# A planner's slots, stores and clock in a fused attention and feed-forward kernel

## The chip, the cores and the metric

The kernel runs on one core of a Trainium2 chip. The metric is the device time of one execution in microseconds (us). The engines are TensorE (PE, matrix products, with PEld for its weight loads), VectorE (DVE), ScalarE (ACT), GpSimd (POOL, which has next to nothing to do here) and SyncE (SP), which issues the DMA transfers; SPq in the profile is SP's queue.

## The reference

```python
S = 448; D = 64                            # 8 batches, 12 heads
scores = q @ k.T / sqrt(D) - log(S)
attn = (1 / (1 + exp(-scores))) @ v        # a sigmoid, no row sum
x = attn, heads side by side               # 3584 tokens x 768
h = max(x @ w_in, 0)                       # w_in: 768 x 2048
g = s * h * h + b                          # s, b: one number each
out = g @ w_out                            # w_out: 2048 x 768
```

Everything is fp32.

## The kernel before, in words

Each fp32 factor of a product is split into a high part and a rest (the low part), both in TensorE's rounded format fp32r, and a product takes three matmuls: high x high, high x low, low x high. The high part is a copy that rounds (ACT, line 1340 for g, 547 for a weight block); the low part is a subtraction from the unrounded value (DVE, through the helper at line 421; 418 is the helper for additions).

The program has three stages in time.

1. Attention, 0 to about 250 us. While it runs, weights are loaded and converted to fp32 blocks (wf), sums over weight blocks are made, and some of them are rounded into tiles t_l_f_g (group g of the row sums of weight block f in layer l) and stored to HBM (wd, line 563 for a base block, 1401 for row sums).
2. The plain block, about 250 to 385 us: the first 512 tokens in the plain form. There are 16 blocks f of 128 hidden channels, taken in the order 0, 8, 1, 9, ... 7, 15. The first layer of a block (ph, line 818, function ffn1, 18 matmuls) and the second layer (po, line 1271, function ffn2, 18 matmuls) alternate on TensorE, each booked with HALF = 4.09 us. Between the two stands the activation: ACT makes r from ph (three passes) and rounds it to g, DVE makes g's low part. Beside this work, the rounded blocks w_l_f (layer l, block f) and the row sums t_0_f_g are made by ACT and DVE and stored by SP, since the third stage reads them back.
3. The fast block, about 385 to 1022 us: the other 6 x 512 tokens, in two groups of three, by a bilinear scheme that needs fewer products and more sums. A unit is 12 matmuls with one set of weights (wu), loaded from wd in HBM (line 918); a_n_mk are tokens, loaded from xd (line 575). Its products (b, lines 1009 and 1018) take operands o_, split into o_..h and o_..l; wr are weight rows that are read back, summed and stored again.

The order of the instructions in the plain block is not written out by hand. A Planner (lines 250 to 325) holds operations, each with an engine, an expected time, the operations it comes after, a number of slots that it needs, and a `late` time. `lag` is how long after its own time an operation counts as done; for a store that is the expected time until it has landed. `deadlines` pulls each `late` forward from its successors. `run` then simulates the engines' clocks: at each step the engine with the earliest possible start takes, of the operations that can start within 0.25 us of one another, the one with the smallest `late`. The result is a fixed order per engine. The chip keeps to it, and waits by semaphores where the real times differ. The planner's clock counts from the start of the plain block: `plan1.clock.update(...)` says when each engine comes free then.

Tiles of first-layer blocks and row sums come from a heap of slots, cx (8 slots "c" and 5 slots "t"). A slot is freed in the plan with a time (`cx.free(tile, at + ...)`), and the next tile takes the slot that stands first in the list. On the chip the first write to a new tile waits until the last reader of the old tile is done, stores among the readers. Second-layer blocks come instead from a ring p2 of three tiles: block i takes the place of block i-3. The plan makes its rounding (ACT) come after the ffn2 of block i-3, and says nothing of that block's store.

`keep` issues the store of a base block. A first-layer tile has two uses (`uses`): its product and its store. Its slot is freed by whichever comes last. `left` (line 1441) does what attention left over on DVE: the low parts of three tiles t_1_1_4, t_1_1_5 and t_1_1_6 (row sums of a second-layer block), and their stores.

At the end of the plain block (the seam) the pools of stages 1 and 2 are closed, and 32 slots of equal size open over the same memory for the fast block. `old` lists the regions of the closed pools with the count at which each was last freed; `h2` orders the 32 new slots by the largest count of the regions below them, so that the first tiles of the fast block go to places that have long been free. In `old` the regions are, in order: 8 slots "c", 4 half-size tiles, 2 small tiles, the 3 tiles of the ring p2, 3 of g, and the 5 slots "t".

Of the kernel before, what the change touches and what calls it, by code (L numbers as in the profile page):

```python
# [36 lines left out]
TB = 512  # L37
# [9 lines left out]
AHEAD_1, AHEAD_R = 16.0, 40.0  # L47
# [281 lines left out]
def sigmoid_attention_relu2_ffn(  # L329
# [17 lines left out]
    KW = DM // 3  # L347
# [10 lines left out]
    def pool(stack, name, bufs, side=None, space=None):  # L358
        kw = dict(side=side) if side else {}
        if space is not None:  # L360
            kw["space"] = space
        return stack.enter_context(
            tc.tile_pool(name=name, bufs=bufs, reuse_waits="tile", **kw)
        )
# [28 lines left out]
    cx = Slots(pool(first, "cx", 1), 8, "c")  # L393
# [3 lines left out]
    early = ExitStack()  # L397
# [16 lines left out]
    def f32(ap):  # L414
        return ap.bitcast(F32)
# [45 lines left out]
    def block(l, f, n):  # L461

        if l == 0:
            return wf[0][f + int(n[1]) * NQ4][:, int(n[0])]
        return wf[1][f + int(n[0]) * NQ4][:, int(n[1])]
# [75 lines left out]
    def base_hi(l, f):  # L541
        shape = [P, 3, 2, KW]
        if l:
            t = p2.tile(shape, F32R, tag="w", name=f"w_{l}_{f}")
        else:
            t = cx.tile(shape, F32R, name=f"w_{l}_{f}")
        nc.scalar.copy(t[:, :, 0], wf[l][f])
        return t

    def base_lo(l, f, t):  # L550
        sub(t[:, :, 1], wf[l][f], f32(t[:, :, 0]))

    def base_rows(l, f):
        part = f // NQ4
        names = [f"{part}{k}" if l else f"{k}{part}" for k in range(3)]
        return [x for x in names if x in ROWS[l]], [k for k in range(3) if names[k] in ROWS[l]]

    def base_store(l, f, t):
        names, thirds = base_rows(l, f)
        f %= NQ4  # L560
        step = thirds[-1] - thirds[0] if len(thirds) == 2 else 1
        row, n = ROWS[l].index(names[0]), len(thirds)
        nc.sync.dma_start(
            wd[l][f // 2][:, row : row + n, f % 2],
            f32(t[:, thirds[0] : thirds[-1] + 1 : step]).rearrange("p k h c -> p k (h c)"),
        )
        kept.update((l, x, f) for x in names)
# [14 lines left out]
    at = ExitStack()  # L582
# [207 lines left out]
    pieces, late = iter(pieces[:-LATE]), pieces[-LATE:]  # L790
# [123 lines left out]
    def fetch():  # L914
        n, l, row, p = stream[len(fetched)]
        assert {(l, row, 2 * p), (l, row, 2 * p + 1)} <= kept, (l, row, p)
        t = roll.tile([P, 2, 2, KW], F32R, tag="wu", name=f"wu_{len(fetched)}")
        nc.sync.dma_start(f32(t).rearrange("p j h c -> p j (h c)"), wd[l][p][:, ROWS[l].index(row)])
        fetched.append(t)
# [332 lines left out]
    for a, *_ in PRODUCTS_1:  # L1252
        seen = [a]
        while seen:
            x = seen.pop(0)
            d = {s_[0]: (s_[1], s_[3]) for s_ in SUMS_1}.get(x)
# [21 lines left out]
    plan1 = Planner(cx)  # L1278
    HALF = 4.09
    w_t, w_lo, g_t, acts, ffns, ph_t = {}, {}, {}, {}, {}, {0: ph0}  # L1280
    row_op, readers, nearly = {}, [], []

    def due(i, l):
        return max(0.0, min(2 * i - 1 + 3 * l, 2 * NF - 1) * HALF)

    def weights(l, i):
        f = order[i]
        uses = [2 - l]

        def drop(at):  # L1290
            uses[0] -= 1
            if not uses[0]:
                cx.free(w_t[l, i], at)

        def run_hi(at):
            w_t[l, i] = base_hi(l, f)

        def keep(at):
            base_store(l, f, w_t[l, i])
            if not l:  # L1300
                drop(at + 5.0)

        h = plan1.op("ACT", 0.76, [ffns.get((1, i - 3))] if l else [], run_hi, 1 - l, early=AHEAD_1)
        d = plan1.op("DVE", 0.89, [h], lambda at: base_lo(l, f, w_t[l, i]))
        k = plan1.op("SP", 0.64 * len(base_rows(l, f)[0]), [d], keep, lag=4.0, late=due(i, l) + 10.0)
        for r in base_rows(l, f)[0]:
            row_op[l, r, f % NQ4] = k
        if f % NP < NP - 1:
            readers.extend((h, d))
        w_lo[l, i] = d, drop  # L1310
# [56 lines left out]
    def weight_sums(f):  # L1367
        tiles = {}

        def new_tile(g):  # L1370
            tiles[g] = cx.tile([P, 3, 2, KW], F32R, name=f"t_0_{f}_{g}")
            return tiles[g]

        jobs = row_sums(0, f, 3, new_tile, lambda x: (lambda: block(0, f, x)), lambda *a: None)
        a, b = ROWS_DUE[f]
        names = [SUM_ROWS[0][k : k + 3] for k in range(0, len(SUM_ROWS[0]), 3)]
        chain = [conv.get(f + NP - NQ4), conv.get(f + NF - NQ4)]
        total = sum(j[1] for j in jobs)
        fresh, his, spent = [], {}, 0.0
        for kind, time, g, fn in jobs:  # L1380
            spent += time
            if kind == "new":
                fresh.append(fn)
            elif kind == "hi":
                his[g] = plan1.op("ACT", 0.04 + 0.24 * len(names[g]), chain, lambda at, fn=fn: fn())
            elif kind == "sum":
                def run(at, fn=fn, first=tuple(fresh)):
                    for x in first:
                        x()
                    fn()  # L1390

                o = plan1.op("DVE", 0.36, chain, run, len(fresh), early=AHEAD_R)
                if f < NQ4 - 1:
                    readers.append(o)
                fresh, chain = [], [o]
            else:
                o = plan1.op("DVE", time, [his[g]] + chain, lambda at, fn=fn: fn())

                def keep(at, g=g):
                    row = ROWS[0].index(names[g][0])  # L1400
                    nc.sync.dma_start(
                        wd[0][f // 2][:, row : row + len(names[g]), f % 2],
                        f32(tiles[g][:, : len(names[g])]).rearrange("p k h c -> p k (h c)"),
                    )
                    cx.free(tiles[g], at + 6.0)
                    kept.update((0, r, f) for r in names[g])

                k = plan1.op("SP", 0.64 * len(names[g]), [o], keep, lag=4.0, late=a + (b - a) * spent / total)
                for r in names[g]:
                    row_op[0, r, f] = k  # L1410
# [3 lines left out]
    for i in range(NF):  # L1414
        weights(1, i)
        if i:
            weights(0, i)
            first_ffn(i)
        activation(i)
        if i:  # L1420
            second_ffn(i - 1)
# [13 lines left out]
    x = None  # L1435
    for k in range(AHEAD):
        _, l, row, p = stream[k]
        after = [o, x] + [row_op.get((l, row, f)) for f in (2 * p, 2 * p + 1)]
        x = plan1.op("SP", 1.28, after, lambda at: fetch(), late=OPEN_DUE + 6.0 + 2.8 * k)
# [5 lines left out]
        stores.clear()  # L1445

    if (NL, "DVE") in plan:
        plan1.op("DVE", 2.4, [], left, late=12.0)
    plan1.full = False
    plan1.clock.update(PE=0.0, DVE=1.0, ACT=-1.0, SP=1.0)  # L1450
    plan1.deadlines()
    plan1.run()
    assert not plan
# [9 lines left out]
    blk.close()  # L1463
    first.close()
    old, at = [], 0
    for tags, size in (("c", 8), 6 * KW), ((None, 4), 3 * KW), ((None, 2), TB), ((None, 3), 6 * KW), ((None, 3), 2 * TB), (("t", 5), 6 * KW):
        for i in range(tags[1]):
            old.append((at, at + size, cx.used[f"{tags[0]}{i}" + "_0" * (tags[0] == "t")] if tags[0] else 0))
            at += size
    size = 2 * TB  # L1470
    h2 = sorted(range(32), key=lambda i: max([u for a, b, u in old if a < (i + 1) * size and b > i * size] or [0]))
# [50 lines left out]
```

## Time and profile before

| | us |
|---|---|
| median of three runs | 1025.07 (1024.07 to 1028.45) |
| the profiled execution | 1024.43 |
| its span | 1022.6 |
| PE busy | 1013.6 (99%) |
| DVE busy | 882.1 (86%) |
| ACT busy | 717.4 (70%) |
| HBM traffic | 272 GB/s over the span |

Busy times are sums over instructions of one engine; the rest of the span is idle time of that engine. In rows of instructions, the first two numbers are start and length in us, then come the engine, the line, the operation, output<-inputs, the shape, and in brackets the idle time just before and what ended it. "DMA wd<-w" as a releaser means that a store of a w tile landed. Rows of a DMA give the time of issue and the time to the landing.

### The profile page before, as it was taken

What the parts mean: (1) busy time and instruction counts of PE and PEld (TensorE: products, weight loads), DVE (VectorE), ACT (ScalarE), POOL (GpSimd) and SP (SyncE); (2) the same over time, 40 slices, a digit from 0 to 9 for tenths busy, and PEclk for the clock granted to TensorE, in tenths of its full rate; (3) what the DMA queues carried; (4) which work ended last, traced back from release to release, by engine and by line L of the source; (5) the groups of instructions that cost most, each with busy time, mean ns of one, the idle gap of its engine ahead of it and who ended that gap; (6) DMA issues with size and microseconds to landing.
All of it is one profiled execution on the core that took longest, in us unless ns stands there. A gap on an engine that the chain in (4) does not pass through costs nothing.

```text
span 1022.6 us, 13811 instructions
## 1 busy us (share of the span) xinstructions
PE 1013.6 (99%) x5194; PEld 761.8 (74%) x5194; DVE 882.1 (86%) x989; ACT 717.4 (70%) x772; POOL 0.2 (0%) x4
## 2 busy tenths in 40 slices
PE   9999999999999999999999999999999999999998
PEld 4545454555788878887887888888888887888887
DVE  5899999998999938989979999899767678999997
ACT  7889999999777747737898954424655889964421
POOL 0000000000000000000000000000000000000000
PEclk9999999999999999999999999999999999999999
DMA  8788999895997998998876666799776666666675
GB/s 338 265 307 300 334 336 391 307 377 222 385 408 308 354 403 303 380 330 275 266 237 186 189 200 189 224 354 326 222 210 194 195 190 189 199 188 199 209 226 186
DMA packets 101073, 278.77 MB, mean 273 GB/s; under 512 B 10000, under 2 KB 23184, under 8 KB 101008
## 3 DMA queue, kind: packets, MB, share of 16 engines
q1 hardware_dynamic: 100720, 277.45, 79.5%
q8 instruction: 41, 0.67, 0.3%
q10 hardware_dynamic: 288, 0.46, 0.1%
q14 instruction: 24, 0.20, 0.1%
HBM read 193.99 MB, written 83.89 MB: 272 GB/s over the span
## 4 chain that ended last, share of the span: by engine, by line
PE 90%; DVE 4%; DMA 3%; ACT 2%; issue 1%; SPq 1%; ACTq 0%; DVEq 0%
PE b L1018 31%; PE b L1009 27%; PE pav L692 10%; PE psc L658 8%; PE po L1271 5%; PE ph L818 4%; PE psc_l L679 2%; PE pav L701 2%; DVE t L421 1%; DVE r L418 1%; DMA wr<-wr 1%; DMA wd<-w 1%; DMA wd<-t 1%; ACT a L638 1%; DVE w L421 0%
## 5 line engine op out<-in xcount | busy, mean ns | idle before, releaser
L1009 PE MATMUL b<-o_0h,wu 128*128 128x512 f32 x928 | 286.5, 389 | 0.7 <-DVE r L421 0.7
L1009 PEld LDWEIGHTS b<-o_0h,wu 128*128 128x128 f32 x928 | 174.2, 188 | 37.9 <-DVE r L421 1.6
L1009 PE MATMUL b<-o_0l,wu 128*128 128x512 f32 x464 | 180.7, 389 | 1.6 <-DVE o_0l L421 1.6
L1018 PE MATMUL b<-o_0h,wu 128*128 128x512 f32 x464 | 152.4, 389 | 0.0
L1018 PE MATMUL b<-o_1h,wu 128*128 128x512 f32 x456 | 149.6, 389 | 0.0
L638 ACT ACTIVATE a<-psc,nls 128x896 f32<-128x896 f32 x144 | 132.7, 1010 | 12.8 <-PE psc L658 10.4
L692 PE MATMUL pav<-a,v 128*64 128x448 f32 x576 | 113.8, 543 | 0.0
L418 DVE TENSOR_TENSOR r<-r,b 128x1024 f32<-128x1024 f32 x74 | 89.4, 1217 | 27.5 <-PE b L1009 17.9
L421 DVE TENSOR_TENSOR r<-r,b 128x1024 f32<-128x1024 f32 x66 | 80.1, 1217 | 25.8 <-PE b L1009 17.0
L1009 PEld LDWEIGHTS b<-o_0l,wu 128*128 128x128 f32 x464 | 87.1, 188 | 19.9 <-DVE o_0l L421 2.0
L1018 PEld LDWEIGHTS b<-o_0h,wu 128*128 128x128 f32 x464 | 87.1, 188 | 18.3 <-ACT r L1064 0.3
L1018 PEld LDWEIGHTS b<-o_1h,wu 128*128 128x128 f32 x456 | 85.6, 188 | 17.9
L1018 PE MATMUL b<-o_0l,wu 128*128 128x512 f32 x232 | 90.3, 389 | 0.0
L1018 PE MATMUL b<-o_1l,wu 128*128 128x512 f32 x228 | 88.7, 389 | 0.0
L692 PEld LDWEIGHTS pav<-a,v 128*64 128x64 f32 x576 | 39.1, 137 | 63.9 <-issue 45.1
L959 ACT CAST o_0h<-r 128x1024 fp32r<-128x1024 f32 x26 | 27.1, 1052 | 67.9 <-DVE r L421 40.0
L1271 PE MATMUL po<-g,w 128*128 128x512 f32 x288 | 68.6, 390 | 2.5 <-ACT g L1340 1.6
L1064 ACT ACTIVATE r<-b 128x1024 f32<-128x1024 f32 x46 | 46.4, 1027 | 31.2 <-DVE r L418 13.8
L1271 PEld LDWEIGHTS po<-g,w 128*128 128x128 f32 x288 | 53.9, 188 | 14.8 <-ACT g L1340 2.0
L491 ACT CAST t<-t 128x768 fp32r<-128x768 f32 (+2 forms) x62 | 44.3, 732 | 29.0 <-DVE t L421 21.7
L818 PE MATMUL ph<-x0h,w 128*128 128x512 f32 x192 | 61.7, 390 | 0.0
L1138 ACT ACTIVATE r<-r,b_sb,s_sb 128x1024 f32<-128x1024 f32 x48 | 59.6, 1243 | 1.0
(115 smaller groups left out, 1693.2 us busy)
## 6 DMA issues: line engine op xcount, KB each, us to landing
wu<-wd SPq DMA_DIRECT2D x232, 512.0 KB, 4.2
wd<-t SPq DMA_DIRECT2D x36, 768.0 KB, 7.0
qk<-qk_t SPq DMA_DIRECT2D x23, 896.0 KB, 6.9
st<-w_out SPq DMA_DIRECT2D x16, 768.0 KB, 8.9
st<-w_in SPq DMA_DIRECT2D x16, 768.0 KB, 9.3
wd<-t SPq DMA_DIRECT2D x22, 512.0 KB, 5.1
v<-v_t SPq DMA_DIRECT2D x24, 448.0 KB, 5.3
xd<-xo SPq DMA_DIRECT2D x24, 448.0 KB, 3.8
```

Source lines behind the costliest of these rows:

```text
L418: nc.vector.tensor_tensor(o, x, y, op=ALU.add)
L421: nc.vector.tensor_tensor(o, x, y, op=ALU.subtract)
L491: nc.scalar.copy(ts[g][:, :n, 0], f32(ts[g][:, :n, 1]))
L638: nc.scalar.activation(a, psc[:, :, :S], AF.Sigmoid, bias=nls, scale=SCALE)
L658: nc.tensor.matmul(o[:, j, :S], two[wi][r, i, cols], two[xi][r, i, :S], start=m == 0, stop=m == 2,)
L692: nc.tensor.matmul(pav[r, i, :S], ld_[1][:, 3 * i + c, j, :], a[i, c][:, j, :], start=c == 0, stop=False,)
L818: nc.tensor.matmul(ph, w[:, k, wi, kc * P : (kc + 1) * P], x0[h][xi][:, cc, :], start=m == 0, stop=m == 3 * NCC - 1,)
L1009: nc.tensor.matmul(bk[:, j], wt[:, j, wi, c * P : (c + 1) * P], tiles[xi][:, c, :], start=first and m == 0, stop=m == 3 * KC - 1, skip_gro ...
L1018: nc.tensor.matmul(bk[:, e], wt[:, f, wi, e * P : (e + 1) * P], tiles[gi][:, f], start=first and f == 0 and m == 0, stop=p == np_ - 1 and ...
L1064: nc.scalar.activation(v.t, bank_t[b], AF.Copy, scale=-1.0)
L1138: nc.scalar.activation(v.t, v.t, AF.Identity, bias=b_sb, scale=s_sb)
L1271: nc.tensor.matmul(pos[e], w[:, k, wi, kc * P : (kc + 1) * P], g[:, gi, :], start=first and i == 0, stop=last and i == 2,)
```

## The change

It changes numbers and dependences of the plain block's planner, and the order in which the places at the seam are taken.

- `keep` of a base block: the store counts as landed 8 us after its issue, not 4. A first-layer tile whose last use is its store is booked as free 8 us after it, not 5. The `late` time of a second-layer store is the block's due time itself, not 10 us later.
- The rounding of second-layer block i comes also after the store of block i-3 (`stored_1`).
- Tiles of row sums are booked as free 8 us after their store, not 6.
- `left` has `late` 20 us, not 12.
- The planner's clock starts with DVE free at 2.8 us and ACT at 0.1, not 1.0 and -1.0.
- At the seam, the three regions of p2 count as freed last of all (tag -1).

```diff
@@ -1278,7 +1278,7 @@
     plan1 = Planner(cx)
     HALF = 4.09
     w_t, w_lo, g_t, acts, ffns, ph_t = {}, {}, {}, {}, {}, {0: ph0}
-    row_op, readers, nearly = {}, [], []
+    row_op, readers, stored_1 = {}, [], {}
 
     def due(i, l):
         return max(0.0, min(2 * i - 1 + 3 * l, 2 * NF - 1) * HALF)
@@ -1298,11 +1298,14 @@
         def keep(at):
             base_store(l, f, w_t[l, i])
             if not l:
-                drop(at + 5.0)
-
-        h = plan1.op("ACT", 0.76, [ffns.get((1, i - 3))] if l else [], run_hi, 1 - l, early=AHEAD_1)
+                drop(at + 8.0)
+
+        before = [ffns.get((1, i - 3)), stored_1.get(i - 3)] if l else []
+        h = plan1.op("ACT", 0.76, before, run_hi, 1 - l, early=AHEAD_1)
         d = plan1.op("DVE", 0.89, [h], lambda at: base_lo(l, f, w_t[l, i]))
-        k = plan1.op("SP", 0.64 * len(base_rows(l, f)[0]), [d], keep, lag=4.0, late=due(i, l) + 10.0)
+        k = plan1.op("SP", 0.64 * len(base_rows(l, f)[0]), [d], keep, lag=8.0, late=due(i, l) + 10.0 * (1 - l))
+        if l:
+            stored_1[i] = k
         for r in base_rows(l, f)[0]:
             row_op[l, r, f % NQ4] = k
         if f % NP < NP - 1:
@@ -1402,7 +1405,7 @@
                         wd[0][f // 2][:, row : row + len(names[g]), f % 2],
                         f32(tiles[g][:, : len(names[g])]).rearrange("p k h c -> p k (h c)"),
                     )
-                    cx.free(tiles[g], at + 6.0)
+                    cx.free(tiles[g], at + 8.0)
                     kept.update((0, r, f) for r in names[g])
 
                 k = plan1.op("SP", 0.64 * len(names[g]), [o], keep, lag=4.0, late=a + (b - a) * spent / total)
@@ -1445,9 +1448,9 @@
         stores.clear()
 
     if (NL, "DVE") in plan:
-        plan1.op("DVE", 2.4, [], left, late=12.0)
+        plan1.op("DVE", 2.4, [], left, late=20.0)
     plan1.full = False
-    plan1.clock.update(PE=0.0, DVE=1.0, ACT=-1.0, SP=1.0)
+    plan1.clock.update(PE=0.0, DVE=2.8, ACT=0.1, SP=1.0)
     plan1.deadlines()
     plan1.run()
     assert not plan
@@ -1463,9 +1466,11 @@
     blk.close()
     first.close()
     old, at = [], 0
-    for tags, size in (("c", 8), 6 * KW), ((None, 4), 3 * KW), ((None, 2), TB), ((None, 3), 6 * KW), ((None, 3), 2 * TB), (("t", 5), 6 * KW):
-        for i in range(tags[1]):
-            old.append((at, at + size, cx.used[f"{tags[0]}{i}" + "_0" * (tags[0] == "t")] if tags[0] else 0))
+    for tag, n, size in (("c", 8, 6 * KW), (0, 4, 3 * KW), (0, 2, TB), (-1, 3, 6 * KW), (0, 3, 2 * TB), ("t", 5, 6 * KW)):
+        for i in range(n):
+            names = (f"{tag}{i}", f"{tag}{i}_0")
+            used = cx.count + 1 if tag == -1 else sum(cx.used[x] for x in names)
+            old.append((at, at + size, used))
             at += size
     size = 2 * TB
     h2 = sorted(range(32), key=lambda i: max([u for a, b, u in old if a < (i + 1) * size and b > i * size] or [0]))
```

TensorE's order is the same in both kernels, and so is the number of instructions on every engine. The following rows are in each engine's order of issue (line, operation, output<-inputs, shape).

DVE at the start of the plain block, before. The wf tiles are unrounded weight blocks, w_0_1 is a rounded one, g_0 the activation of the first block.

```order
L421 TENSOR_TENSOR w_0_1_2736<-wf_0_1_102,w_0_1_2736 128x3x256
L421 TENSOR_TENSOR t_0_0_0_2746<-wf_0_4_114,wf_0_12_116 128x256
L421 TENSOR_TENSOR t_1_1_5_2579<-t_1_1_5_2579 128x3x256
L421 TENSOR_TENSOR t_1_1_4_2479<-t_1_1_4_2479 128x3x256
L421 TENSOR_TENSOR t_1_1_6_2583<-t_1_1_6_2583 128x256
L421 TENSOR_TENSOR t_0_0_0_2746<-wf_0_8_100,wf_0_12_116 128x256
L418 TENSOR_TENSOR t_0_0_0_2746<-t_0_0_0_2746 128x256
L421 TENSOR_TENSOR g_0_2774<-r_0_2775,g_0_2774 128x512
```

The same place, after:

```order
L421 TENSOR_TENSOR w_0_1_2736<-wf_0_1_102,w_0_1_2736 128x3x256
L421 TENSOR_TENSOR t_0_0_0_2771<-wf_0_4_114,wf_0_12_116 128x256
L421 TENSOR_TENSOR t_0_0_0_2771<-wf_0_8_100,wf_0_12_116 128x256
L418 TENSOR_TENSOR t_0_0_0_2771<-t_0_0_0_2771 128x256
L421 TENSOR_TENSOR t_0_0_0_2771<-wf_0_0_98,t_0_0_0_2771 128x256
L421 TENSOR_TENSOR t_0_0_1_2778<-wf_0_4_114,wf_0_8_100 128x256
L421 TENSOR_TENSOR g_0_2764<-r_0_2765,g_0_2764 128x512
```

The three low parts of t_1_1_4 to t_1_1_6 no longer stand ahead of g_0; small sums of t_0_0_0 and t_0_0_1 do. The low parts come further down DVE's order, after:

```order
L421 TENSOR_TENSOR g_8_2803<-r_8_2804,g_8_2803 128x512
L418 TENSOR_TENSOR t_0_0_2_2839<-wf_0_0_98,wf_0_8_100 128x256
L421 TENSOR_TENSOR t_1_1_5_2579<-t_1_1_5_2579 128x3x256
L421 TENSOR_TENSOR t_1_1_4_2479<-t_1_1_4_2479 128x3x256
L421 TENSOR_TENSOR t_1_1_6_2583<-t_1_1_6_2583 128x256
L421 TENSOR_TENSOR t_0_0_1_2778<-t_0_0_1_2778 128x3x256
```

They stand behind g_8, the second activation. Seven rows below the last of these comes the first write of t_0_0_3, which has the slot of t_1_1_5.

SP near the end of the plain block, before. wu_u are the weights of unit u of the fast block, wd_l_p weight rows in HBM, a_0_mk tokens.

```order
L918 DMA wu_4_3736<-wd_0_0_91 128x1024
L1401 DMA wd_0_1_92<-t_0_3_5_3631 128x3x512
L563 DMA wd_1_1_94<-w_1_6_3473 128x2x512
L575 DMA a_0_01_3763<-xd_1_84 128x2x384
L575 DMA a_0_01_3763<-xd_2_85 128x2x128
```

The store of w_1_6 stands behind the loads of units 0 to 4. After:

```order
L918 DMA wu_0_3619<-wd_0_0_91 128x1024
L1404 DMA wd_0_1_92<-t_0_3_3_3587 128x3x512
L563 DMA wd_1_1_94<-w_1_6_3467 128x2x512
L575 DMA a_0_21_3661<-xd_3_86 128x2x256
L575 DMA a_0_21_3661<-xd_4_87 128x2x256
L918 DMA wu_1_3669<-wd_0_1_92 128x1024
```

It now stands behind the load of unit 0, 15 rows earlier in SP's order, with the loads of units 1 to 4 behind it. w_1_15 takes the place of w_1_6 in the ring.

At the seam, in the order in which the 32 new slots are taken, slots 16 to 20 lie over the three tiles of p2. Before, they are the fifth to ninth; after, they are the last five. The instructions behind the seam have the same order in both kernels; their tiles lie in other places.

## The prediction

> **What bounds the kernel now.** I read the page first, then the waits of TensorE (PE), then PE's instructions in order of time at each of its stalls, and from there back along the chain of waits.
>
> ```profile
> span 1022.6 us, 13811 instructions
> PE 1013.6 (99%) x5194; PEld 761.8 (74%) x5194; DVE 882.1 (86%) x989; ACT 717.4 (70%) x772; POOL 0.2 (0%) x4
> wd<-w SPq DMA_DIRECT2D x20, 512.0 KB, 5.8
> ```
>
> PE is busy 99% of the span, and the order of its instructions is the same in both kernels. So the change can win only what PE stands idle, and lose only by making it idle. PE's waits, longest first (engine, line, what released it: total, times, longest):
>
> ```profile
> PE b L1009 <- DVE o_0l L421: 1.6, 1, 1.6
> PE po L1271 <- ACT g L1340: 1.6, 1, 1.6
> PE po L1271 <- DVE g L421: 0.9, 2, 0.7
> ```
>
> These are three places. From PE's instructions (start, length, idle time in brackets):
>
> ```profile
> 259.15 0.39 PE L1271 MATMUL po<-g,w 128*128 128x512 f32 x1
> 260.26 2.11 PE L1271 MATMUL po<-g,w 128*128 128x512 f32 x8 [0.73 <-DVE g L421]
> ...
> 374.41 4.24 PE L1271 MATMUL po<-g,w 128*128 128x512 f32 x18
> 380.21 0.51 PE L1271 MATMUL po<-g,w 128*128 128x512 f32 x1 [1.56 <-ACT g L1340]
> 380.94 4.16 PE L1271 MATMUL po<-g,w 128*128 128x512 f32 x17 [0.22 <-DVE g L421]
> 384.94 0.39 PE L1009 MATMUL b<-o_0h,wu 128*128 128x512 f32 x1
> ...
> 466.31 0.61 PE L1009 MATMUL b<-o_0h,wu 128*128 128x512 f32 x2
> 468.50 0.50 PE L1009 MATMUL b<-o_0l,wu 128*128 128x512 f32 x1 [1.57 <-DVE o_0l L421]
> ```
>
> In the run of 18, matmuls start (4.24-0.39)/17 = 0.227 us apart. What each stall costs beyond that pace: A, at the start of the plain block, 260.26-259.15-0.23 = 0.88 us. B, at its end, 380.21-(374.41+18x0.227) = 1.72, and 380.94-380.21-0.23 = 0.50, together 2.22 us. C, in the fast block, 468.50-466.31-2x0.227 = 1.74 us. All three come to 4.84 us, 0.47% of the time: that is nearly all the change can reach.
>
> **The change part by part.** No instruction is added or removed; everything below is order, dependence and place.
>
> *Stall A: VectorE's later start, and the moved rounding of the left-over row sums.* VectorE (DVE) and ScalarE (ACT) there:
>
> ```profile
> 256.32 0.42 DVE L421 TENSOR_TENSOR t<-wf,wf 128x256 f32<-128x256 f32 x1
> 256.66 2.16 DVE L421 TENSOR_TENSOR t<-t 128x768 fp32r<-128x768 f32 x3
> 258.73 0.42 DVE L421 TENSOR_TENSOR t<-wf,wf 128x256 f32<-128x256 f32 x1
> 259.18 0.43 DVE L418 TENSOR_TENSOR t<-t 128x256 f32<-128x256 f32 x1
> 259.53 0.68 DVE L421 TENSOR_TENSOR g<-r,g 128x512 fp32r<-128x512 f32 x1
> 257.41 0.62 ACT L1340 CAST g<-r 128x512 fp32r<-128x512 f32 x1
> ```
>
> The high part of g_0 is there at 257.41+0.62 = 258.03; DVE turns to the low part only at 259.53, since the three left-over low parts (258.73-256.66 = 2.07 us) stand ahead. In the new order they stand behind g_8, and five small sums stand ahead of g_0. From 256.32, at the 0.34 us between the starts at 256.32 and 256.66, they are done at 258.02. So g_0's low part starts with its high part, near 258.1, and ends 0.7 later, at 258.8. PE asks for it with its second matmul, 259.15+0.23 = 259.38: 0.6 us to spare. A goes: -0.88.
>
> What is late instead: t_1_1_5 (rows left over from attention) is stored later, and the planner still books its slot as free at once. Behind its low part on DVE stands the next tile in that slot, t_0_0_3. A low part of 768 elements takes DVE 0.87 (2.07 for two and a small one of 0.34), a g 0.68. Between the two stand five such low parts, three small sums and g_1: 5x0.87+3x0.34+0.68 = 6.05 us. The nearest rows for a landing are those of all stores of w and of row sums in the block (min/median/max):
>
> ```profile
> DMA to landing us min/median/max: 2.7/6.0/10.9
> DMA to landing us min/median/max: 2.7/6.3/10.4
> ```
>
> Landing after 2.7 us gives no wait, after 10.9 one of 4.9 us; I take 2.7, from the landing of 8.78 in the full queue shown below. It lies on DVE. Queued behind it are the low parts of g_9 and of the later g's, and PE waits for those. Before, these rows:
>
> ```profile
> 279.49 0.69 DVE L421 TENSOR_TENSOR g<-r,g 128x512 fp32r<-128x512 f32 x1 [0.43 <-ACT g L1340]
> 284.81 4.08 PE po L1271 x18
> ```
>
> g_9 is done 284.81-(279.49+0.69) = 4.6 us before PE needs it, and DVE idled 0.43 before it. In the new order a low part of w_1_2 and three small sums, 1.9 us, no longer stand ahead of g_9. With PE 0.88 earlier DVE may lose 4.6+0.4+1.9-0.9 = 6.0 us. So PE loses 0, at either bound; past that cover each further microsecond costs PE one.
>
> *The longer holds (5 and 6 become 8 us) elsewhere.* They remove waits such as ACT's 1.93 us below; ACT is idle 30% of the span and no PE stall lies near: 0. New tiles begin later in the plan for it, but by the same count over DVE's two orders every later g has no more work ahead of it than before: 0.
>
> ```profile
> 283.38 0.84 ACT L547 CAST w<-wf 128x768 fp32r<-128x768 f32 x1 [1.93 <-DMA wd<-t]
> ```
>
> *Stall B: the second-layer block waits for its predecessor's store.* The chain of waits into B, and ACT's row before it:
>
> ```profile
> 359.65 8.20 DMA wd<-t
> 367.86 8.78 DMA wd<-w
> ...
> 366.45 0.60 ACT L1337 ACTIVATE r<-ph 128x512 f32<-128x512 f32 x1 [4.70 <-PE ph L818]
> 368.59 0.62 ACT L1340 CAST g<-r 128x512 fp32r<-128x512 f32 x1
> 376.67 0.83 ACT L547 CAST w<-wf 128x768 fp32r<-128x768 f32 x1 [7.46 <-DMA wd<-w]
> 369.25 0.69 DVE L421 TENSOR_TENSOR g<-r,g 128x512 fp32r<-128x512 f32 x1 [6.70 <-ACT g L1340]
> 354.65 0.36 SPq L1401 DMA_DIRECT2D wd<-t  x1
> ```
>
> ACT could have rounded w_1_15 at 369.21 but waits until the store of w_1_6, its predecessor in the ring of three, has landed; r_15 stands behind it on ACT, then g_15, then PE. Undisturbed, r_15 starts with ph_15's end near 374.6 (r_7 started at 366.45, 0.2 after PE had gone on at 374.41-36x0.227 = 366.24; for r_15 PE goes on at 374.41), its high part ends 2.76 later (366.45 to 369.21) at 377.4, its low part 3.49 later (to 369.94) at 378.1. PE asks at 378.49 and 378.72: no stall, 0.6 us to spare. For that the store must land by 373.7, a rounding (0.83) before r_15.
>
> In the new order this store stands 15 rows earlier on SP, right behind that of t_0_3_3, which went out at 354.65. Between then and 367.86 lie 13 us. With the 8.78 of the row above it lands near 364, with the worst landing, 10.9, and some 2 us of SP's own waits near 368: 5 us inside the limit. Bounds of the term: 0 (it lands past 376.6 again) and -2.22; I take -2.22, since both landings lie far inside. What it is moved ahead of, the tokens and the weights of the first units, goes 1.3 us later (512 KB at the 401 GB/s of these windows: stretch, PE, PEld, DVE, ACT and POOL busy, clock, DMA share, GB/s):
>
> ```profile
> 366.00:376.00 10.00, 10.00 (x46) 8.26 (x44) 0.69 (x1) 2.67 (x4) 0.00 (x0) 1.00 1.05 401
> 401.00:406.00 5.00, 5.00 (x23) 4.13 (x22) 4.97 (x10) 4.68 (x6) 0.00 (x0) 1.00 0.52 163
> ```
>
> Unit u of the fast block starts at 384.94+2.72u (12 matmuls each), so u = 6 at 401.3. The eighth load of weights waits for unit 0's end, 387.7, and the first seven stand ahead of it: even one that left only then would be there 10.9 later, at 398.6. Covered.
>
> A rule stands against this term. The Trainium skill ("DMA: Bandwidth & Descriptors", section "Anatomy of one DMA", fitted there on the GpSimd path) puts a transfer at 2.0 us plus its bytes at 436 GB/s: an estimate of 3.2 us for 512 KB. By it the store of 367.86 lands at 371.1, inside the limit, so moving it wins nothing: 1023.5 by the rule, 1021.3 by the row. The trace shows 8.78 with the DMA engines full (share 1.05); the measurement decides.
>
> *The places at the seam.* The slots over the three w tiles are taken last. Now the third sum of the fast block lands on one:
>
> ```profile
> 390.17 1.23 DVE L421 TENSOR_TENSOR s_None<-a,s_None 128x1024 f32<-128x1024 f32 x1 [3.53 <-DMA wd<-w]
> 392.52 1.22 DVE L968 SCALAR_TENSOR_TENSOR o_0l<-s_None,o_0h 128x1024 fp32r<-128x1024 f32 x1
> ```
>
> The 3.53 us go. But the operand that hangs on it was done at 393.74, and its unit, u = 4, starts at 395.82; PE did not wait. Worth 0 between 0 and 0. The slot it takes instead lies over g tiles that PE reads until its last po matmul, at 384.9; DVE came there at 390.17-3.53 = 386.6: no wait.
>
> *Stall C.* Its chain begins at loads whose issue PE paces:
>
> ```profile
> 442.62 0.53 SPq L1178
> 443.92 8.86 DMA wr<-wr
> 467.31 1.14 DVE o_0l L421
> 439.54 1.22 DVE L421 TENSOR_TENSOR r<-r,b 128x1024 f32<-128x1024 f32 x1 [0.47 <-PE b L1009]
> ```
>
> At 439.54 DVE has caught up with PE, and at 401 to 406 the DMA queue had run dry (share 0.52 above): what is won at the seam does not reach here. The order behind the seam is unchanged. 0, at best -1.74, at worst 2 more if the landing takes the longest of the rows above, 10.9.
>
> **Sum.** -0.88-2.22 = -3.10 on the profiled execution's 1024.43 (span 1022.6 and 1.83 around it): 1021.3. That execution is 0.64 below the median of the runs, 1025.07 (1024.07 to 1028.45); I add a third of it and say 1021.5. About 0.5% (5 us) is what a measurement of this kernel can tell from no change.
>
> **The rivals.** Only A goes (the rounding of w_1_15 still comes after 376, behind some other store): 1024.43-0.88 = 1023.5. For it: SP is held by landings all along there. Against: 5 us of room. The page's rule above would end here too.
> C goes as well: 1024.43-4.84 = 1019.6. For it: DVE is 3.5 us freer after the seam. Against: the 0.47 us wait for PE at 439.54 wipes that out.
> Slower: t_0_0_3's wait for t_1_1_5's store outgrows its cover. It decides from 6.0 us of wait on, a landing 6.05+6.0 = 12 us after the issue, and outweighs the 3.1 won from 15 us on; 18 us give 1021.3+6 = 1027.3. For it: the slot is booked free at once and DMA is full. Against: no store in the block took over 10.9.
>
> **How the numbers follow.** Forecast 0.70, only A 0.13, C too 0.10, slower than before 0.05, others 0.02. The range takes the first two and half of C's case: 1019.6 to 1024.0. Faster by over 0.5% is below 1019.9: the C case, 0.10. Slower by over 0.5% (above 1030.2) needs a landing of 21 us: 0.02. The rest, 0.88, is within 0.5%.
>
> **What would show it.** A: no PE idle at the first po. B: ACT rounds w_1_15 near 369, no wait for wd<-w, and PE runs po into b without a gap. Seam: no DVE wait for wd<-w near 390. C: the same 1.6 us behind o_0l. New: a DVE wait of some 3 us for wd<-t near 270. I am wrong if PE shows a stall between 262 and 375, or if C moves.

## The result and the profile after

The changed kernel takes 1020.87 us (median of 8 runs, 1020.16 to 1021.69), the kernel before, in 8 runs beside it, 1025.86 (1023.27 to 1028.63). The ratio is 0.9948, with a 95% interval of 0.9932 to 0.9964: about half a per cent faster. The predicted time was 1021.5, in a range of 1019.6 to 1024.0. The profiled executions are 1024.43 before and 1021.23 after, a difference of 3.20; the sum of the prediction was 3.10. The medians differ by 5.0. So there are two things to explain: whether the 3.2 are made of the terms that were forecast, and where the medians have their other 1.8 from.

The head of the page of the changed kernel (the span; busy time, share and count of each engine):

```profile
span 1019.5 us, 13816 instructions
PE 1013.4 (99%) x5194; PEld 762.0 (75%) x5194; DVE 882.2 (87%) x989; ACT 718.4 (70%) x772; POOL 0.2 (0%) x4
```

No work went away; PE's busy time is the same to 0.2 us, and the 3.1 us of the span were idle time. The waits of PE, after:

```profile
PE b L1009 <- DVE o_0l L421: 1.2, 2, 0.6
...
PE b L1009 <- DVE r L421: 0.7, 2, 0.4
```

Both waits of po (g from ACT, g from DVE) are gone. Of o_0l there are now two, where there was one of 1.6 us. PE's instructions at the old places and at the new one (start, length, idle time in brackets):

```profile
259.35 4.24 PE L1271 MATMUL po<-g,w 128*128 128x512 f32 x18
...
373.59 8.32 PE L1271 MATMUL po<-g,w 128*128 128x512 f32 x36
381.75 0.39 PE L1009 MATMUL b<-o_0h,wu 128*128 128x512 f32 x1
...
397.84 0.61 PE L1009 MATMUL b<-o_0h,wu 128*128 128x512 f32 x2
398.98 0.50 PE L1009 MATMUL b<-o_0l,wu 128*128 128x512 f32 x1 [0.52 <-DVE o_0l L421]
...
463.96 0.61 PE L1009 MATMUL b<-o_0h,wu 128*128 128x512 f32 x2
465.21 0.50 PE L1009 MATMUL b<-o_0l,wu 128*128 128x512 f32 x1 [0.64 <-DVE o_0l L421]
```

ACT's rounding of w_1_15, which had waited 7.46 us for the store of w_1_6, waits for nothing any more:

```profile
368.31 0.83 ACT L547 CAST w<-wf 128x768 fp32r<-128x768 f32 x1
```

The first po (A) and the last two (B: 36 matmuls in one piece, then b without a gap) run unbroken. At 398 there is a stall that the kernel before does not have, call it D; at 464 stall C is smaller. Each as the distance between two starts less 0.227 us for each matmul between them:

| stall | before | after | forecast after |
|---|---|---|---|
| A, first po | 0.88 | 0 | 0 |
| B, last po | 2.22 | 0 | 0 |
| D, 398 us | 0 | 0.69 | 0 |
| C, 464 us | 1.74 | 0.80 | 1.74 |
| sum | 4.84 | 1.49 | 1.74 |

PE lost 3.35 us less; attention, which the change does not touch, took 0.2 longer in this execution. C gained by about what D cost, and the sum came out near the forecast with two errors of opposite sign in it.

What ended D, in the changed kernel (DVE, SP's issues with their counts, and a piece of the chain of waits), and what the same places were before (the last two lines):

```profile
397.21 0.42 DVE L421 TENSOR_TENSOR t<-wr 128x256 f32<-128x256 f32 x1 [5.81 <-DMA wr<-wr]
397.70 1.23 DVE L421 TENSOR_TENSOR o_0l<-s_None,o_0h 128x1024 fp32r<-128x1024 f32 x1
385.04 4.64 SPq L1178 DMA_DIRECT2D wr<-wr  x3
386.86 10.26 DMA wr<-wr
...
396.89 0.43 DVE L421 TENSOR_TENSOR t<-wr 128x256 f32<-128x256 f32 x1 [0.75 <-DMA wr<-wr]
388.27 1.95 SPq L1178 DMA_DIRECT2D wr<-wr  x3
```

The reads of raw weight rows (wr) went out 3.2 us earlier, as PE is earlier, and were there no earlier: 397.2 after, 396.9 before. The windows of the DMA queue there (stretch, PE, PEld, DVE, ACT and POOL busy, clock, DMA share, GB/s; after, then before):

```profile
388.00:390.00 2.00, 2.00 (x11) 1.65 (x10) 0.00 (x0) 2.00 (x3) 0.00 (x0) 1.00 1.04 412
394.00:398.00 4.00, 4.00 (x19) 3.34 (x18) 0.73 (x2) 2.30 (x3) 0.00 (x0) 1.00 1.04 418
...
388.00:390.00 2.00, 2.00 (x11) 1.65 (x10) 0.00 (x0) 0.00 (x0) 0.00 (x0) 1.00 0.91 273
```

Before, the queue was not full for a moment when the wr reads came (273 GB/s). After, it is full, and the three stores of w tiles that went out from 379.6 on take 9.6 to 10.9 us to land. The profiles of the runs below bear this out. In nine of them, these two counted, the first of the reads went out between 382.0 and 388.3 us and VectorE waited for it until 395.1 to 397.2, with little regard to when it went out. In three others PE was so late that the reads went out after 390, when the queue had emptied (DMA shares of 0.51, 0.24 and 0.02 in windows of 2 us there); in these the wait ended between 398.9 and 400.4. So a PE that is 3 us earlier meets the landing at nearly the same time.

### The profile page after: what moved, and what is told of

It is laid out like the page before. It is cut to its first block, busy times and chain, and to the rows that moved or that the text cites. A ratio compares the mean times of both kernels' runs of the same rounds, so it can differ in the third digit from the quotient of the medians.

```text
span 1019.5 us, 13816 instructions
## 1 busy us (share of the span) xinstructions
PE 1013.4 (99%) x5194; PEld 762.0 (75%) x5194; DVE 882.2 (87%) x989; ACT 718.4 (70%) x772; POOL 0.2 (0%) x4
## 4 chain that ended last, share of the span: by engine, by line
PE 89%; DVE 6%; DMA 2%; ACT 1%; issue 1%; SPq 0%; DVEq 0%; ACTq 0%
PE b L1018 31%; PE b L1009 22%; PE pav L692 11%; PE psc L658 9%; PE ph L818 6%; PE po L1271 6%; PE psc_l L679 2%; PE pav L701 2%; DVE t L421 1%; DVE r L418 1%; DMA wr<-wr 1%; DVE r L421 1%; DMA wu<-wd 1%; DVE o_0l L421 1%; DVE o_0l L968 1%
```

## The experiments

Every run that follows was timed beside the kernel before on its chip. In the three groups of runs the kernel before had medians of 1026.26, 1026.47 and 1026.69; the changed kernel itself was not run again, and its 1020.87 beside 1025.86 is what they are set against. The kernel before differs by up to 0.8 us from group to group, so a difference of about 1 us or less between two variants rests on their profiles more than on their medians.

**The clock and the left-over sums alone (A).**

```diff
-        plan1.op("DVE", 2.4, [], left, late=12.0)
+        plan1.op("DVE", 2.4, [], left, late=20.0)
-    plan1.clock.update(PE=0.0, DVE=1.0, ACT=-1.0, SP=1.0)
+    plan1.clock.update(PE=0.0, DVE=2.8, ACT=0.1, SP=1.0)
```

> Before, with only the planner's clock (DVE 2.8, ACT 0.1) and the late time of the left-over row sums (20) changed. Stall A (0.88 us) goes by every theory. Theory 1 (the prediction's sum: the terms are independent): the kernel is 0.9 us faster, median near 1025.0, and stall B stays 2.2 us. Theory 2 (the store of w_1_6, which ends stall B, is paced by the DMA queue and not by PE): PE comes to B 0.9 us earlier and waits for the same landing, B grows to 3.1 us, median unchanged near 1025.9. By both, the runs keep the range of some 5 us that the kernel before has, if that range comes from B.

1027.75 us (11 runs, 1026.56 to 1029.13) against 1026.26; ratio 1.0013, interval 1.0003 to 1.0023. Stall A is gone, and the kernel is slower. The rows of B (a piece of the chain, ACT, PE, and the clock in a window):

```profile
369.76 8.90 DMA wd<-w
378.69 0.83 ACT L547 CAST w<-wf 128x768 fp32r<-128x768 f32 x1 [10.43 <-DMA wd<-w]
373.45 4.24 PE L1271 MATMUL po<-g,w 128*128 128x512 f32 x18
382.22 6.81 PE L1271 MATMUL po<-g,w 128*128 128x512 f32 x18 [4.53 <-ACT g L1340]
384.00:386.00 2.00, 2.00 (x6) 1.61 (x5) 2.00 (x3) 1.85 (x2) 0.00 (x0) 0.50 1.02 407
```

PE comes to B 1.0 us earlier, and the landing that it waits for comes 2.0 us later than before (378.66 against 376.64). The store itself goes out later, at 369.76 instead of 367.86: the edit moves rows of SP too (a store of another w tile now stands at 362.41, among the loads ahead of it). Theory 1 (terms that can be added up) falls. Theory 2 is right in that the landing does not follow PE, but not in its sizes: B is 382.22-(373.45+18x0.227) = 4.68 us long instead of 3.1, and the median is not unchanged. And something more shows: behind the 4.5 us wait the granted clock is 0.50, and 18 matmuls take 6.81 us. In the profile of the kernel before the same 18, with their second wait, took 4.89 (from 380.21 to 385.10).

**The late time of second-layer stores alone (B).**

```diff
-        k = plan1.op("SP", ..., [d], keep, lag=4.0, late=due(i, l) + 10.0)
+        k = plan1.op("SP", ..., [d], keep, lag=4.0, late=due(i, l) + 10.0 * (1 - l))
```

> Before, with only the late time of the second-layer stores changed (10 us earlier), so that the store of w_1_6 goes out some 23 rows of SP earlier. Theory 1: B goes whole (2.2 us) without the new dependence on the store and without anything else, A stays 0.9 us, median near 1023.6. Theory 3 (the kernel before loses more at B in most runs than the 2.2 us of its profiled run): median near 1022, and the range of the runs shrinks from 5 us to the 1.5 us of the changed kernel. Rival: the early rounding of w_1_15 waits for another landing and B stays, 1025.9.

1022.92 us (1022.56 to 1023.77) against 1026.26; ratio 0.9968, interval 0.9956 to 0.9981. One expression wins 3.3 us, more than the 2.2 of theory 1 and less than the 3.9 of theory 3, and the spread of the runs shrinks from 5.5 to 1.2, as theory 3 has it. ACT rounds w_1_15 14 us earlier and waits for no store:

```profile
362.91 0.84 ACT L547 CAST w<-wf 128x768 fp32r<-128x768 f32 x1 [0.63 <-PE po L1271]
```

**The old places at the seam, in the changed kernel.**

```diff
-    for tag, n, size in (("c", 8, 6 * KW), ..., (-1, 3, 6 * KW), ...):   # p2 taken last
+    for tags, size in (("c", 8), 6 * KW), ..., ((None, 3), 6 * KW), ...: # as before
```

> The changed kernel with the old order of places at the seam. Theory 1 (the prediction: the place is worth 0): same as the changed kernel, 1020.9, since the wait for the store of the w tile was covered. Theory 2 (the landing at the seam is paced by the DMA queue, whereas PE now comes 3 us earlier): VectorE waits for the store until about 390 us, the operand of unit 4 is done near 394 while PE wants it at 392.7: a stall of 1 to 1.5 us, 1022 to 1022.4.

1022.28 us (1021.77 to 1024.74); 1.4 above the changed kernel. Its rows (DVE, ACT, PE), and the row of ACT before as the last line:

```profile
389.45 1.23 DVE L421 TENSOR_TENSOR s_None<-a,s_None 128x1024 f32<-128x1024 f32 x1 [6.73 <-DMA wd<-w]
390.71 1.06 ACT L961 ACTIVATE o_0h<-s_None 128x1024 fp32r<-128x1024 f32 x1 [7.46 <-DVE s_None L421]
392.57 1.02 ACT L1064 ACTIVATE r<-b 128x1024 f32<-128x1024 f32 x1
393.65 0.50 PE L1009 MATMUL b<-o_0h,wu 128*128 128x512 f32 x1 [1.16 <-ACT r L1064]
...
391.43 1.06 ACT L961 ACTIVATE o_0h<-s_None 128x1024 fp32r<-128x1024 f32 x1 [4.27 <-DVE s_None L421]
```

The store lands at 389.4 here and landed at 390.2 before: the landing stays, PE has moved, and the wait grew from 3.53 to 6.73 us. PE does not stall at the operand, as was expected, but at a bank: ACT's emptying of the banks (r, line 1064) stands behind the rounding that hangs on the late sum. The distance between the two starts of PE there (392.10 and 393.65) is 1.32 us more than its pace. The run of the late time alone, which has the old places too, shows the same stall with 0.71 us. So the edit that was priced at 0 is worth some 1.4 us, once the others have moved PE.

**A longer planned landing of the wr reads, in the changed kernel.**

```diff
-            return v, plan3.op("SP", 0.06, [], run, 1, early=6.0, lag=5.0)
+            return v, plan3.op("SP", 0.06, [], run, 1, early=6.0, lag=10.0)
```

> The changed kernel, with the load of raw weight rows behind the seam planned as 10 us instead of 5, so that VectorE takes the first sum of them behind the operand of unit 6 instead of ahead of it, and SP issues these loads one or two rows earlier. If the new stall of 0.68 us at 398 us is only that row standing ahead of the operand: it goes, 1020.2, and the stall at 464 us stays between 0 and 0.8. Rival: VectorE then waits at the same landing with the next operand behind it, and PE stalls one unit later by as much: 1020.9.

1019.83 us (1019.47 to 1020.20); ratio to the kernel before 0.9936, interval 0.9922 to 0.995. It is 1.0 below the changed kernel, the ranges of the two hardly touch, and both D and C are gone from its profile; PE's list of waits holds nothing of o_0l. DVE in this run:

```profile
391.37 1.22 DVE L421 TENSOR_TENSOR o_0l<-s_None,o_0h 128x1024 fp32r<-128x1024 f32 x1
395.10 0.42 DVE L421 TENSOR_TENSOR t<-wr 128x256 f32<-128x256 f32 x1 [2.51 <-DMA wr<-wr]
```

The operand now stands ahead of the sum that waits, and the reads, a row earlier on SP, land at 395.1. DVE still idles 2.5 us there, which nobody needs.

**The late time put back, the dependence kept.**

```diff
-        k = plan1.op("SP", ..., [d], keep, lag=8.0, late=due(i, l) + 10.0 * (1 - l))
+        k = plan1.op("SP", ..., [d], keep, lag=8.0, late=due(i, l) + 10.0)
```

> The changed kernel with the late time of the second-layer stores put back (10 us later), the dependence of the rounding on the store three blocks before kept. The store of w_1_6 is then late on SP again, as before the change, but the plan puts r_15 ahead of the rounding of w_1_15 on ACT. If ACT's order were the fault in stall B, it is gone: 1020.9. If the late landing is (the theory from the run with the clock alone, where it came at 378.7 us): PE wants w_1_15 at 377.6, its high part is there at 379.5 and its low part at 380.5, a stall of some 2 to 2.5 us instead of 4.7: 1023 to 1023.5.

1022.30 us (1021.65 to 1024.15), 1.4 above the changed kernel. The stall is at the rounded weight itself (the chain, ACT, and PE's waits):

```profile
368.04 9.87 DMA wd<-w
377.94 0.83 ACT L547 CAST w<-wf 128x768 fp32r<-128x768 f32 x1 [1.63 <-DMA wd<-w]
PE po L1271 <- ACT w L547: 1.2, 1, 1.2
...
PE po L1271 <- DVE w L421: 0.3, 1, 0.3
```

By the starts of its matmuls (18 from 373.35, two from 378.82, the rest from 379.81) PE loses 1.38 + 0.54 = 1.92 us there instead of 4.7 with A alone. The store landed at 377.91, 0.8 us earlier than with A alone, so not all of this is the dependence; but r_15 now stands ahead of the rounding, and PE waits for the weight and no longer for g. So the dependence helps when the store is late; it does not replace the earlier store.

**The holds put back (4, 5 and 6 us).**

```diff
-                drop(at + 8.0)
+                drop(at + 5.0)
-        k = plan1.op("SP", ..., [d], keep, lag=8.0, ...)
+        k = plan1.op("SP", ..., [d], keep, lag=4.0, ...)
-                    cx.free(tiles[g], at + 8.0)
+                    cx.free(tiles[g], at + 6.0)
```

> The changed kernel with the holds put back: stores count as landed after 4 us, slots of first-layer tiles come free after 5 and of row sums after 6. The prediction's sum gives them 0: 1020.9, within 0.5. Rival: tiles begun earlier in the plan put DVE or ACT behind a store that has not landed (as ACT's 1.93 us wait before), in front of a g that PE wants: up to 2 us slower, 1023.

1021.35 us (1020.73 to 1021.67), 0.5 above the changed kernel, with ranges that overlap; its profile shows only stall C (0.77 us). No stall in the plain block came back. The holds are worth nothing that these runs can tell.

**The dependence taken out, the late time kept.**

```diff
-        before = [ffns.get((1, i - 3)), stored_1.get(i - 3)] if l else []
+        before = [ffns.get((1, i - 3)), ] if l else []
```

> The changed kernel without the dependence of a second-layer rounding on the store three blocks before; the earlier late time of the stores is kept. The rounding of w_1_15 then stands 4 rows earlier on ACT, ahead of r_7. If the earlier store alone takes stall B away (as in the run of the late time alone): same as the changed kernel, 1020.9. Rival: the rounding waits for the landing, near 363 us, with r_7 behind it, and PE stalls at the second layer of block 7 by up to 2 us: 1022 to 1023.

1020.83 us (1020.25 to 1021.19): the same. With the store early, the dependence does nothing.

**The longer planned landing of the wr reads on the kernel before.** The edit is the one shown above (`lag=5.0` becomes `lag=10.0`), made on the old kernel.

> The kernel before, with only the planned time of the raw weight row loads behind the seam raised from 5 to 10 us. If stall C (1.74 us) is a matter of the order of VectorE against these landings, it goes here too, without the change: 1024.3 against 1026.0. Rival: C comes from the DMA queue and stays, 1026.0. Stalls A and B stay by both.

1025.83 us (1023.22 to 1028.16) against 1026.47; ratio 0.9992, interval 0.9979 to 1.0005. In its profile stall C fell from 1.74 to 0.25, but the median shows less than half of that. So the run does not settle what C is worth in the kernel before; B's scatter is larger. Its profile shows B once more (PE, and the clock in two windows):

```profile
375.01 4.24 PE L1271 MATMUL po<-g,w 128*128 128x512 f32 x18
381.06 0.51 PE L1271 MATMUL po<-g,w 128*128 128x512 f32 x1 [1.81 <-ACT g L1340]
381.79 5.75 PE L1271 MATMUL po<-g,w 128*128 128x512 f32 x17 [0.22 <-DVE g L421]
382.00:384.00 2.00, 2.00 (x6) 1.57 (x6) 2.00 (x3) 1.04 (x1) 0.00 (x0) 0.56 1.06 419
384.00:386.00 2.00, 2.00 (x7) 1.54 (x7) 2.00 (x3) 1.96 (x4) 0.00 (x0) 0.59 1.03 405
```

Here a B of 1.96 + 0.50 us is followed by a clock of 0.50, for 3.41 us, and the last 18 matmuls take 6.48 us with their second wait instead of 4.89.

**Useless matmuls in stall B of the kernel before.**

```diff
+    fill = ps_h.tile([P, TB], F32, tag="ph", name="fill")
+    for i in range(8):
+        nc.tensor.matmul(fill, g_t[NF - 2][:, 0, :P], g_t[NF - 2][:, 0, :], start=i == 0, stop=i == 7)
     ffn2(w_t[1, NF - 1], g_t[NF - 1], False, True)
```

> The kernel before with 8 useless matmuls (8 x 0.227 = 1.8 us of TensorE work, into a free bank, read by nobody) put between the second layers of blocks 7 and 15, that is into stall B. Clock theory (in most runs of the kernel before, stall B lets TensorE's granted clock fall to a half for 3.4 or 6.8 us afterwards, which costs 1.6 us or more): the matmuls fill the wait, the clock stays at 1.0 in nearly all runs, and more work makes the kernel faster: median 1024.7 to 1025 against 1026.3, range 1023.4 to 1027. Rival (the lost time is the landing alone, the lower clock only goes along with it): unchanged 1026.3 if the stall covers the matmuls, up to 1028 if it does not.

1025.06 us (11 runs, 1023.80 to 1027.19) against 1026.69 (15 runs); ratio 0.9982, interval 0.997 to 0.9994. More work on the busiest engine made the kernel 1.6 us faster, by the medians. Its rows:

```profile
379.04 1.98 PE L1459 MATMUL fill<-g 128*128 128x512 f32 x8
382.11 0.50 PE L1271 MATMUL po<-g,w 128*128 128x512 f32 x1 [1.10 <-ACT g L1340]
382.84 4.15 PE L1271 MATMUL po<-g,w 128*128 128x512 f32 x17 [0.23 <-DVE g L421]
```

The wait did not become shorter: the last po starts 3.07 us behind PE's pace (382.11 instead of 379.04), more than in any profile of the kernel before, but with the matmuls in it, and the clock behind it is 1.0. The mean clock over the span is 1.0 (to the third digit, or 0.999) in 10 of these 11 runs, and 0.998 in one. In the 15 runs of the kernel before beside it, it was 1.0 once.

**A undone in the changed kernel** (clock DVE 1.0, ACT -1.0; `late=12.0`).

> The changed kernel with the planner's old clock (DVE 1.0, ACT -1.0) and the old late time (12) of the left-over row sums. Stall A (0.88 us) is back. Theory: A is worth its 0.9 us once stall B no longer stands behind it, though alone it won nothing: 1021.8 against 1020.9. Rival: what A wins is given back to the DMA queue at 398 and 464 us (stalls 0.68 and 0.80): the same as the changed kernel, 1020.9.

1021.92 us (1021.00 to 1024.94), 1.05 above the changed kernel, with ranges that overlap; stall A is back with 0.88. This agrees with the theory that A is worth its 0.9 once B is gone. Alone it is worth nothing, or less; in its one profile the store at B went out later with it.

**Four edits alone:** A, the late time, the places at the seam, and the wr reads at 10 us, on the kernel before; no holds, no dependence.

> The kernel before with four edits alone: the planner's clock and the late time of the left-over sums (A), the earlier late time of second-layer stores (B), the places at the seam, and the planned landing of the raw weight rows (10 us). The dependence on the store and the longer holds are left out. If these two are worth nothing: the same as the changed kernel with the longer planned landing, 1019.8. Rival: up to 0.5 us slower, 1020.3.

1019.83 us (1019.55 to 1021.21); ratio 0.9939, interval 0.9926 to 0.9953. The same as with holds and dependence. Of the versions that were run, this has the fewest edits among those with a median below both kernels.

**The kernel before once more, for a second profile.**

> The kernel before once more, for a second profile of it. Clock theory: if its time is above 1025.7, the row of the clock shows a half for 3.4 or 6.8 us right behind stall B, and the matmuls of the last second layer take 1.6 us or more above 4.16; if it is below 1025.7, the clock is 1.0 throughout and stall B is under 2.2 us.

One run, 1025.18 us. PE at B, and the clock there:

```profile
374.36 4.24 PE L1271 MATMUL po<-g,w 128*128 128x512 f32 x18
380.77 6.16 PE L1271 MATMUL po<-g,w 128*128 128x512 f32 x18 [2.17 <-ACT g L1340]
...
378.00:382.00 4.00, 1.83 (x5) 0.95 (x4) 2.21 (x3) 2.62 (x5) 0.00 (x0) 0.85 1.05 408
382.00:386.00 4.00, 4.00 (x14) 3.12 (x13) 4.00 (x5) 3.30 (x5) 0.00 (x0) 0.72 1.04 411
```

The wait ahead of B's first matmul is 2.33 us instead of 1.72, and now the clock falls to a half for 3.41 us, from 380.81 on. The last 18 matmuls take 6.16 us; with their second wait alone they took 4.89 before, so the lower clock costs 1.3. The forecast for this run was missed: a time below 1025.7 was to go with a clock of 1.0 throughout. Other stalls move the total too (C was 0.58 here), so the total alone does not tell whether the clock fell.

## Why the prediction was right, and where not

**A and B, the terms of the sum: right in place and size for one execution.** PE runs unbroken at both places; ACT rounds w_1_15 at 368.31 ("near 369"). The store of w_1_6 went out at 354.24 and landed 7.4 us later, at 361.6 (forecast: near 364). B is due to the one expression in `late`: alone it takes B away, without it B comes back (1.92 us, with the dependence kept). That the store moves 15 rows forward on SP was the right thing to price. The longer holds were priced at nothing, and no run tells them from nothing; the dependence has no price of its own in the prediction, and without it the time is the same.

**Against the rule that was weighed there:** the Trainium skill ("DMA: Bandwidth & Descriptors", "Anatomy of one DMA", a fit on the GpSimd path) would have had the store landed after an estimated 3.2 us, and moving it worth nothing. Moving it alone won 3.3 us, and the landings at this place took 8.4 to 9.9 us in six executions (8.42 in the second profile of the kernel before, 9.87 in the run without the late time). The DMA engines were full there, at a share of 1.05 (366 to 376 us, kernel before); the size of the transfer alone does not give its time.

**"Worth 0 between 0 and 0", the places at the seam: wrong.** They are worth some 1.4 us. Two steps failed. The slack of the operand was read off the old times of PE (395.82), although the same text moves PE 3.1 us forward, to 392.7, which is ahead of the 393.74 at which the operand was done. And behind DVE's wait only the operand was followed; ACT's queue, where the emptying of the banks stands behind the rounding, was not. In the total it does not show, since the changed kernel has the edit.

**"Covered", what the store is moved ahead of: wrong by the reads behind the weights.** The weights of units were checked, the wr reads that follow them on SP were not; they met a queue that was still full, and D costs 0.69 in the profiled execution. It is a close matter: in three other profiles with the same order on DVE (holds put back, dependence taken out, A undone) VectorE waits 5.10, 5.12 and 3.04 us for the same reads, and PE shows no wait there. In both runs in which the plan expects the landing 10 us after the issue the operand stands ahead of the sum that waits, and D is gone.

**C: it moved, which the prediction had named as a sign of being wrong.** It was held to be untouched because PE paces the issue of its reads. The issue did move with PE (440.27 against 442.62), but the reads landed after 5.2 to 7.2 us instead of 7.0 to 8.9, and VectorE no longer waited for them; why they were quicker no run shows. C differs between executions of one kernel, too: 1.74 and 0.58 in two of the kernel before, 0.80 after. After, it is a different wait, for a store of row sums:

```profile
463.93 1.23 DVE L421 TENSOR_TENSOR o_0l<-a,o_0h 128x1024 fp32r<-128x1024 f32 x1 [0.61 <-DMA wd<-t]
```

**The new wait of some 3 us on DVE near 270: did not come.** t_0_0_3 starts at 271.13, right behind g_9, which had waited 0.64 for ACT. The stores of the three left-over tiles landed 3.4 to 4.7 us after their issue, where the prediction took the 8.78 of another place; that is within the 6 us that were counted as the way between them.

**From the profiled execution to the median: right by luck.** The prediction took the profiled execution as 0.64 below the median and added a third. In 50 more runs of the kernel before the median is 1026.56. The mean clock was 1.0 in 10 of them, with a median of 1024.7, and 0.995 to 0.998 in 40, with a median of 1026.95. The profiled execution, at clock 1.0, was one of the rare ones. Against those ten alone the changed kernel is 3.8 us faster. So most of what the change wins in the median beyond the 3.1 of the sum goes with the lower clock behind B, which the useless matmuls kept up without shortening the wait. Some of it may be a longer B: its first wait was 1.96, 2.33 and 3.07 us in three later profiles with the old order of the stores, against 1.72; how long it is in the runs without a profile is not on record. The changed kernel is not hit by the lower clock (1.0 in all 8 runs), so its own forecast time was close, while the gain of 5.0 us came out larger than the 3.1 of the sum. In per cent that is 0.52, just past the 0.5 to which the prediction gave a chance of 0.10; the interval, 0.36 to 0.68, lies on both sides of it.

The rule on the clock that bears on this stands in the Trainium skill ("TensorE: Matmul & The Clock Gate", "What's actually happening"): the clock is halved after an idle window, and windows are 3.4 us long and run on by themselves. The runs agree on the halving and on the length (3.41 us twice, 6.83 once). What counts as an idle window the section does not say; here it need not be idle throughout. In the second profile of the kernel before, 2.17 us of unbroken idle time (378.60 to 380.77), with 1.2 us of matmuls ahead of it in the last 3.41, were enough, and in the profile of the longer planned landing on the kernel before 1.81 + 0.22 us. In the first profile of the kernel before 1.56 + 0.22 us were not. How much idle time of a window it takes, no run here settles.

## What to carry to other kernels

When a change moves the busiest engine forward, ask of every transfer near it whether its landing moves too: here, landings out of a full DMA queue stayed nearly where they were, and stalls that are ended by them grew by up to as much as was won ahead of them. So gains at two places do not add up until the last one that a landing ends has been taken away, and an edit that looks worthless on the old times can be needed on the new ones. Look also at the clock of the profiled execution against that of the other runs before taking its idle time for the price of a stall.

## What the hardware showed that was not expected

- A wait of PE can cost more than its length. Waits of 1.72 + 0.50 us left the clock at 1.0; 1.96 + 0.50 and 2.33 + 0.50 brought it to 0.50 for 3.41 us (1.6 and 1.3 us more), and 4.68 us for 6.83 us (1.9 us more). With 1.9 us of stall left (late time put back) 1 of 7 runs had a mean clock of 0.998 or less, with the kernel before 40 of 50, with A alone 11 of 11. One of 6 runs with the old places at the seam and one of 5 with A undone had it too, though their profiled executions show no stall above 1.32 us; what lowered the clock in those two runs is not known.
- Filling the wait with matmuls that nobody reads won 1.6 us in the median. The clock stayed up in 10 of 11 of those runs, while the wait itself, in the one that was profiled, was not shorter.
- A 512 KB store of the same line took 5.8 us in the median of the kernel before and 8.4 to 9.9 us at B, where the DMA engines were full.
